# Two more head pairs and four raw weight pieces placed in layer 1's accumulators at the start, pieces in another order, first narrow unit behind the fourth pair

## The chip, the cores and the metric

One core of one Trainium2 chip runs the whole program. The metric is the device time of one execution in microseconds (us), as the median of several runs. Engines are named as in the profile: PE (TensorE matmul), PEld (its weight loads), DVE (VectorE), ACT (ScalarE), POOL (GpSimd), SP (the queue that issues nearly all DMAs).

## The reference, cut to what matters

A retention layer (attention without softmax, with a decay per head) feeds two feed-forward layers. The two layers' weights are float64, all else float32.

```python
# q, k, v: (4 batches, 8 heads, 576 tokens, 64), float32
scores = (1 / 8) * q @ k^T
D[i, j] = gamma[head] ** (i - j) if i >= j else 0
x = (scores * D) @ v                     # -> (2304 tokens, 512)
h = x @ w1_in;  g = max(0.01 * h, h);  x = g @ w1_out   # 512 -> 2048 -> 512
h = x @ w2_in;  g = h - tanh(h);       out = g @ w2_out
```

## The kernel before

**Retention** works on 16 head pairs (4 batches of 4 pairs; a pair fills the 128 partitions with 2 x 64). For pair i the four loads are `qT`, `kT` (288 KB each), `kn` (256 KB) and `vn` (320 KB), all issued by SP. Then: `prep(i)` on POOL scales the queries (L373) and the values (L378); `prep_tail(i)` on DVE scales the 64 last queries (L386), and ACT copies them into the tile `bd` (L390); `scores(i)` on PE (L401, L407) gives `sc` and `x_a`; `mask(i)` on DVE (L416, L423) turns these into `pt`; `states_mm(i)` on PE (L434) writes the products of each chunk into one PSUM tile `x_c`, and `states(i)` on ACT (L444) and DVE (L448, six instructions) adds them up with decay into `st`; `outputs_far` and `outputs_near` on PE (L465, L477) form the output from `st` and `pt`, in the PSUM tile `o` and, for the 64 last tokens, in a corner of `x_c`; `finish` splits the output into a high half `xh` (ACT, L486) and a low half `xl` (DVE, L487).

**Weights** come in pieces of 128 x 512 float64 (512 KB). A piece is loaded raw (`load_piece`, L109), narrowed to float32 by five steps (`narrow_ops`: an absolute value on ACT, L127; then on DVE a clamp, L137, a shift, L142, and two joins, L148), and split into a high and a low half (`split_piece`: ACT L174, POOL L175) in the tile `wp`. Two raw pieces fit in the pool `stage`, and two narrowed ones in the pool `cw` of this stage, so a third piece begins when the first has been split. The first eight pieces (four of layer 1's `w_in`, four of `w_out`) are narrowed during retention.

**Units.** From the sixth pair on, half of a block of 256 tokens of layer 1's first group is slipped in with each pair: `unit_h` (24 matmuls, L518, into the tile `x_b`), a leaky ReLU twice on ACT (L525, L526), the low half on POOL (L527), and `unit_o` (24 matmuls, L543), which is issued one pair later. There are 12 units. After every second one `unit_evac` copies sums into `acc`, an SBUF tile of 128 x 9216 float32 that accumulates layer 1's output. Until then `acc` holds nothing.

**Order.** No scheduler moves anything: each engine does its instructions in the order in which the code is written. In the loop over pairs it is load, prep of the next pair, scores, mask, prep_tail of the next pair, a part of the pieces' steps (`fill`), `pair_steps`, another part. The table `at_pair` says how many of the steps in the list `ops` are done by the end of each pair, a third of them at each of the up to three calls of `fill`. Behind retention `layers` runs layer 1's remaining blocks and layer 2, with PE as the engine that never rests (L194, L266).

Of the kernel before, what the change touches and what calls it, by code (L numbers as in the profile page):

```python
# [10 lines left out]
F32 = mybir.dt.float32  # L11
F32R = mybir.dt.float32r
U32 = mybir.dt.uint32
I64 = mybir.dt.int64
# [4 lines left out]
P = 128  # L19
# [14 lines left out]
def retention_moe_moe(  # L34
# [16 lines left out]
    nc = tc.nc  # L51
    B, NP, _, S = qT.shape
# [3 lines left out]
    NFULL = S // CH  # L56
    TAIL = S - NFULL * CH
    NCH = NFULL + 1
# [6 lines left out]
    stage = ctx.enter_context(tc.tile_pool(name="stage", bufs=2))  # L65
# [36 lines left out]
    cw_pool = [None]  # L102
    early = [True]

    def load_piece(key):
        m, kind, f = key
        src = ((w1i, w1o), (w2i, w2o))[m][kind][f]
        st = stage.tile([P, 512], I64 if wide else F32, tag="st", name="st")
        nc.sync.dma_start(out=st, in_=src)  # L109
        raw[key] = st  # L110

# [68 lines left out]
    def pieces_of(m, g):  # L180
        return [(m, kind, g * GF + f) for f in range(GF) for kind in range(2)]
# [125 lines left out]
    def split_order(keys):  # L307

        return sorted(keys, key=lambda k: (k[2] + LAG * k[1], k[1]))

    def piece_ops(keys, split=True, spare=()):


        ops, late = [], []
        for j, key in enumerate(keys):
            part = narrow_ops(key)
            if j + 2 < len(keys):
                part.append(lambda k=keys[j + 2]: load_piece(k))
            ops += part[:3] + late + part[3:]
            late = [lambda k=key: split_piece(k)] if split else []  # L320
            if key in spare:
                late = [lambda k=key: keep_piece(k)]
        return ops + late


    def retention():
        with ExitStack() as ac:
# [20 lines left out]
            qk, kv, pts = {}, {}, {}  # L348
            order = [(b, p) for b in range(B) for p in range(NP)]

            def load(i):
                load_qk(i)
                load_v(i)

            def load_qk(i):
                b, p = order[i]
                t = ap_.tile([P, 2, S], F32, tag="qk", name="qk")
                nc.sync.dma_start(out=t[:, 1, :], in_=qT[b, p])
                nc.sync.dma_start(out=t[:, 0, :], in_=kT[b, p])
                qk[i] = t  # L360

            def load_v(i):
                b, p = order[i]
                t = ap_.tile([P, NFULL + NCH, P], F32, tag="kv", name="kv")
                nc.sync.dma_start(out=t[:, :NFULL, :], in_=kn[b, p])
                nc.sync.dma_start(out=t[:, NFULL:, :], in_=vn[b, p])
                kv[i] = t
# [114 lines left out]
            def finish(i, ot):  # L482
                b, p = order[i]
                for src, lo, hi in ((o_tail, MAIN, S), (ot, 0, MAIN)):
                    ts = slice(b * S + lo, b * S + hi)
                    nc.scalar.activation(out=xh[:, p, ts], in_=src, func=AF.Copy)  # L486
                    nc.vector.tensor_tensor(  # L487
                        out=xl[:, p, ts], in0=src, in1=xh[:, p, ts].bitcast(F32), op=ALU.subtract
                    )


            pieces = split_order(pieces_of(0, 0))
            ops = piece_ops(pieces)
            at_pair = [3, 8, 14, 21, 30, 44, 54]
            first = NP + 1
            done, u = [0], 0

            def fill(i, part):
                a, b = ([0] + at_pair + [len(ops)] * len(order))[i:i + 2]
                now = a + (b - a) * (part + 1) // 3  # L500
                for op in ops[done[0]:now]:
                    op()
                done[0] = max(done[0], now)
# [7 lines left out]
            def unit_h(u):  # L511
                t0, f0 = place(u)
                for f in range(2):
                    w = wt[0, 0, f0 + f]
                    for kk in range(KK):
                        cs = slice(kk * P, (kk + 1) * P)
                        for j, (wi, x) in enumerate(((0, xh), (0, xl), (1, xh))):
                            nc.tensor.matmul(  # L518
                                out=x_b[:, f, :], lhsT=w[:, wi, cs], rhs=x[:, kk, t0:t0 + QW],
                                start=f == 0 and kk == 0 and j == 0,  # L520
                                stop=f == 1 and kk == KK - 1 and j == 2, skip_group_check=True,
                            )
                a = t0_.tile([P, 2, QW], F32, tag="u", name="a")
                gt = g0_.tile([P, 2, 2, QW], F32R, tag="g", name="g")
                nc.scalar.activation(out=a, in_=x_b, func=AF.Prelu, alpha=0.01)  # L525
                nc.scalar.activation(out=gt[:, 0], in_=x_b, func=AF.Prelu, alpha=0.01)  # L526
                nc.gpsimd.tensor_tensor(  # L527
                    out=gt[:, 1], in0=a, in1=gt[:, 0].bitcast(F32), op=ALU.subtract
                )
                gs[u] = gt  # L530

            def unit_o(u):
                t0, f0 = place(u)
                gt = gs.pop(u)
# [15 lines left out]

            def unit_evac(u):
                t0, f0 = place(u)
                if f0 == 0:
                    return
                ps = accs.pop(u // 2)
                dst = acc_t[:, :, t0:t0 + QW]
                nc.scalar.activation(out=dst[:, 2:], in_=ps[:, 2:], func=AF.Copy)
                nc.vector.tensor_copy(out=dst[:, :2], in_=ps[:, :2])

            def pair_steps(i, fast):  # L560

                nonlocal u
                if fast:
                    unit_h(u)
                    fill(i, 1)
                    if u:
                        unit_o(u - 1)
                        unit_evac(u - 1)
                    u += 1
                if i:  # L570
                    ot = outputs_far(i - 1)
                    outputs_near(i - 1, ot, [NFULL])
                    outputs_near(i - 1, ot, range(NFULL))
                    del pts[i - 1], kv[i - 1]
                if i < len(order):
                    states_mm(i)
                if i:
                    finish(i - 1, ot)
                if i < len(order):
                    states(i)  # L580

            t = ap_.tile([P, 2, S], F32, tag="qk", name="qk")
            nc.sync.dma_start(out=t[:, 1, :], in_=qT[0, 0])
            nc.scalar.dma_start(out=qt_sb[:, 0, :], in_=qtab[:, 0, :])
            nc.sync.dma_start(out=t[:, 0, :], in_=kT[0, 0])
            qk[0] = t
            nc.scalar.dma_start(out=cm_sb, in_=cmask)
            nc.scalar.dma_start(out=vt_sb, in_=vtab)
            nc.scalar.dma_start(out=qt_sb[:, 1:, :], in_=qtab[:, 1:, :])
            load_v(0)  # L590
            load_qk(1)
            load_piece(pieces[0])
            load_v(1)
            nc.vector.memset(qb[:, 2:3], 0.0)
            nc.vector.memset(qb[:, 0:1], -RHO_V * math.sqrt(RHO_C))
            nc.vector.memset(qb[:, 1:2], -TANH_T * TANH_T)
            nc.scalar.activation(out=qb[:, 3:4], in_=qb[:, 2:3], func=AF.Tanh)
            for t in sts + bds:
                nc.vector.memset(t, 0.0)
            load_piece(pieces[1])  # L600
            prep(0)
            prep_tail(0)
            for i in range(len(order)):
                if i + 2 < len(order):
                    load(i + 2)
                fast = i >= first
                if i + 1 < len(order):
                    prep(i + 1)
                sc = scores(i)
                scores_tail(i)  # L610
                mask(i, sc)
                if i + 1 < len(order):
                    prep_tail(i + 1)
                fill(i, 0)
                pair_steps(i, fast)
                fill(i, 2)
            pair_steps(len(order), True)
            assert done[0] >= len(ops)
            unit_o(u - 1)
            unit_evac(u - 1)  # L620
            assert 2 * u == n_early


    def layers():
# [135 lines left out]
```

## Time and profile before

| | before |
|---|---|
| median of 3 runs | 895.46 us (894.61 to 895.62) |
| profiled execution, first to last instruction (its span) | 893.7 us |
| what lies around the span, median less span | 1.8 us |
| PE busy | 868.6 us, 97% |
| DVE, ACT, POOL busy | 541.6, 378.0, 421.2 us |
| head of the program, 0 to 80 us: PE busy | 58.85 us |
| 80 to 160 us: PE busy | 80.00 us |
| 160 us to the end (733.7 us): PE busy | 729.75 us |

The profiled execution has only its span as a time of its own; a median belongs to it by adding the 1.8 us that lie around. Read the profile by stages: PE is busy without a gap from 80 us on, and nearly all of its idle time lies in the first 80 us, where the pairs and the first pieces are worked through. A row of the timeline gives start, duration, engine, line, operation, the tiles written and read, and in brackets how long the engine had been idle and what released it.

### The profile page before, as it was taken

To read this page: it belongs to the slowest core of one execution; us is meant where nothing else is said; L and a number is where in the kernel's file an instruction comes from. 1 tells how busy PE (TensorE), PEld (TensorE's weight loads), DVE (VectorE), ACT (ScalarE), POOL (GpSimd) and SP (SyncE) were. 2 spreads that over 40 slices of the span, in tenths; PEclk is the share of its full clock that TensorE was granted. 3 is DMA by queue.
4 is the path that set the end of the run, shared out by engine and by line. 5 is a ranking of instruction groups with operands and counts; after the bars stand their busy time and mean duration, and the time that the engine had idled before them with its cause. 6 is when DMAs were issued, how large, how long until landed. Compare 5 with 4: busy or idle time off the path is not lost.

```text
span 893.7 us, 13252 instructions
## 1 busy us (share of the span) xinstructions
PE 868.6 (97%) x5024; PEld 747.0 (84%) x5024; DVE 541.6 (61%) x922; ACT 378.0 (42%) x767; POOL 421.2 (47%) x340
## 2 busy tenths in 40 slices
PE   6869999999999999999999999999999999999998
PEld 5759999988888889888888888888888888888886
DVE  6864544698898787865662544444545555555454
ACT  2333232232222321232324666675566555565553
POOL 4544342265223622264224654585457744585443
PEclk9789999999999999999999999999999999999999
DMA  7634432132365335631120200020001000001111
GB/s 276 230 124 131 137 107 101 48 118 95 132 186 166 107 118 157 186 106 47 48 83 24 61 12 1 0 72 24 1 1 43 17 1 1 1 1 48 48 48 70
DMA packets 28574, 70.95 MB, mean 79 GB/s; under 512 B 3296, under 2 KB 3680, under 8 KB 28512
## 3 DMA queue, kind: packets, MB, share of 16 engines
q1 hardware_dynamic: 27936, 69.74, 23.7%
q8 instruction: 39, 0.64, 0.3%
q10 hardware_dynamic: 576, 0.38, 0.1%
q14 instruction: 23, 0.19, 0.1%
HBM read 59.10 MB, written 11.01 MB: 78 GB/s over the span
## 4 chain that ended last, share of the span: by engine, by line
PE 92%; DMA 2%; DVE 2%; POOL 1%; ACT 1%; issue 1%; SPq 0%; POOLq 0%; ACTq 0%
PE h L194 40%; PE a L266 40%; PE a L543 4%; PE x_b L518 3%; DMA kv<-in_vn 2%; PE sc L401 1%; PE o L477 1%; PE o L465 1%; POOL wp L175 1%; PE x_c L434 1%; PE x_a L407 0%; POOL kv L378 0%; DVE cw L148 0%; DVE cw L142 0%; PE x_c L477 0%
## 5 line engine op out<-in xcount | busy, mean ns | idle before, releaser
L194 PE MATMUL h<-xh,wp 128*128 128x512 f32 (+1 forms) x1184 | 355.3, 366 | 0.0
L194 PEld LDWEIGHTS h<-xh,wp 128*128 128x128 f32 x1184 | 216.1, 188 | 36.9
L194 PE MATMUL h<-xl,wp 128*128 128x512 f32 (+1 forms) x592 | 216.9, 366 | 0.0
L266 PE MATMUL a<-wp,g 128*128 128x512 f32 x864 | 209.4, 390 | 0.2 <-POOL g L240 0.2
L266 PEld LDWEIGHTS a<-wp,g 128*128 128x128 f32 x864 | 161.0, 188 | 33.8 <-POOL g L240 1.0
L266 PE MATMUL a<-g,wp 128*128 128x512 f32 (+1 forms) x816 | 175.6, 364 | 0.0
L240 POOL TENSOR_TENSOR g<-v,g 128x512 fp32r<-128x512 f32 (+1 forms) x80 | 94.9, 1186 | 144.6 <-ACT g L239 144.5
L266 PEld LDWEIGHTS a<-g,wp 128*128 128x128 f32 x816 | 141.4, 189 | 24.6
L240 POOL TENSOR_TENSOR g<-a,g 128x512 fp32r<-128x512 f32 (+1 forms) x68 | 87.5, 1286 | 154.5 <-ACT g L208 141.1
L207 ACT ACTIVATE a<-h 128x512 f32<-128x512 f32 (+1 forms) x68 | 37.3, 548 | 227.1 <-PE h L194 226.1
L175 POOL TENSOR_TENSOR wp<-cw,wp 128x512 fp32r<-128x512 f32 x64 | 91.1, 1432 | 82.8 <-ACT wp L174 82.5
L194 PEld LDWEIGHTS h<-xl,wp 128*128 128x128 f32 x592 | 111.6, 189 | 18.6
L233 DVE TENSOR_TENSOR h<-h,t 128x512 f32<-128x512 f32 (+1 forms) x80 | 51.5, 644 | 107.3 <-ACT t L217 107.3
L148 DVE SCALAR_TENSOR_TENSOR cw<-st,cw 128x512 uint32<-128x512 uint32 x128 | 113.3, 885 | 4.0
L292 DVE TENSOR_TENSOR acc<-a,acc 128x512 f32<-128x512 f32 (+1 forms) x114 | 74.0, 662 | 68.3 <-PE a L266 68.1
L239 ACT ACTIVATE g<-v 128x512 fp32r<-128x512 f32 (+1 forms) x80 | 47.2, 589 | 145.4 <-DVE v L237 144.3
L218 POOL TENSOR_TENSOR v<-t,u 128x512 f32<-128x512 f32 (+1 forms) x80 | 94.7, 1184 | 14.2 <-ACT t L217 13.8
L234 DVE SCALAR_TENSOR_TENSOR v<-q,v 128x512 f32<-128x512 f32 (+1 forms) x80 | 55.5, 694 | 55.2 <-POOL v L218 54.2
L237 DVE COPY_PREDICATED v<-mk,h 128x512 f32<-128x512 uint32 (+1 forms) x80 | 54.8, 685 | 9.2 <-DVE v L234 1.4
L219 ACT ACTIVATE q<-u,qb 128x512 f32<-128x512 f32 (+1 forms) x80 | 54.5, 681 | 0.0
L222 ACT ACTIVATE mk<-u,qb 128x512 f32<-128x512 f32 (+1 forms) x80 | 54.2, 678 | 0.0
L131 DVE TENSOR_SCALAR cw<-st 128x512 uint32<-128x512 uint32 x56 | 40.5, 724 | 18.6 <-DMA st<-in_w2i 6.4
(60 smaller groups left out, 803.7 us busy)
## 6 DMA issues: line engine op xcount, KB each, us to landing
st<-in_w1i SPq DMA_DIRECT2D x16, 512.0 KB, 3.3
st<-in_w1o SPq DMA_DIRECT2D x16, 512.0 KB, 3.2
st<-in_w2i SPq DMA_DIRECT2D x16, 512.0 KB, 3.8
st<-in_w2o SPq DMA_DIRECT2D x16, 512.0 KB, 3.8
kept<-cw SPq DMA_DIRECT2D x24, 256.0 KB, 4.1
cw<-kept SPq DMA_DIRECT2D x24, 256.0 KB, 2.6
kv<-in_vn SPq DMA_DIRECT2D x16, 320.0 KB, 5.2
qk<-in_qT SPq DMA_DIRECT2D x16, 288.0 KB, 3.4
```

Of the source, the lines that this page charges most:

```text
L148: nc.vector.scalar_tensor_tensor(out=t["w"], in0=t[src], scalar=scalar, in1=t["w"], op0=op, op1=ALU.bitwise_or)
L175: nc.gpsimd.tensor_tensor(out=wp[:, 1, :], in0=wf, in1=wp[:, 0, :].bitcast(F32), op=ALU.subtract)
L194: nc.tensor.matmul(out=ps[:, :n], lhsT=w[:, wi, cs], rhs=x[:, kk, t0:t0 + n], start=kk == 0 and i == 0, stop=kk == KK - 1 and i == 2,)
L218: nc.gpsimd.tensor_tensor(out=v[:, :n], in0=t_[:, :n], in1=u[:, :n], op=ALU.mult)
L219: nc.scalar.activation(out=q[:, :n], in_=u[:, :n], func=AF.Square, scale=math.sqrt(RHO_C), bias=qb[:, 0:1])
L222: nc.scalar.activation(out=mk[:, :n], in_=u[:, :n], func=AF.Relu, bias=qb[:, 1:2])
L233: nc.vector.tensor_tensor(out=h, in0=h, in1=t_, op=ALU.subtract)
L234: nc.vector.scalar_tensor_tensor(out=v, in0=q, scalar=RHO_A, in1=v, op0=ALU.add, op1=ALU.mult)
L237: nc.vector.copy_predicated(out=v, mask=mk.bitcast(U32), data=h)
L240: nc.gpsimd.tensor_tensor(out=gt[:, 1, :n], in0=v, in1=gt[:, 0, :n].bitcast(F32), op=ALU.subtract)
L266: nc.tensor.matmul(out=o, lhsT=l, rhs=r, start=f == 0 and i == 0 and d % pack == 0, stop=f == GF - 1 and i == 2 and (d + 1) % pack == 0, s ...
L292: nc.vector.tensor_tensor(out=dst, in0=a, in1=dst, op=ALU.add)
```

## The change

- Pairs 3 and 4 are loaded into `acc` (columns 4608 to 9215) and four raw pieces too (columns 0 to 4095), so that five pairs and six pieces are asked for at once at the start. `piece_ops` gets a parameter `ahead`: piece j + 6 is loaded behind piece j, where it was j + 2.
- In the loop pair i + 4 is loaded for i up to 1 and pair i + 2 after that, where the number is over 4. This names pair 5 twice, at i = 1 and at i = 3; both loads are issued, and the second is the one that is read.
- The pieces come as in 0, in 1, out 0, out 1, in 2, in 3, out 2, out 3; it was in 0, in 1, in 2, out 0, in 3, out 1, out 2, out 3.
- `at_pair` is 6, 12, 14, 18, 34, 50 (of 50 steps, loads among them); it was 3, 8, 14, 21, 30, 44, 54 (of 54).
- `first` is 4 in place of 5: the first `unit_h` stands with the fifth pair's states, behind the fourth pair's `finish`.
- `pair_steps` is in another order: outputs and `finish` of the last pair, `unit_o` and `unit_evac`, a part of the steps, then `states_mm` and `states`, then `unit_h`. It was `unit_h`, steps, `unit_o`, `unit_evac`, outputs, `states_mm`, `finish`, `states`. The `unit_o` that stood alone at the end of retention is gone into the loop's last `pair_steps`.

```diff
-    def load_piece(key):
+    def load_piece(key, at=None):
...
+        elif wide:
+            st = acc[:, at:at + 1024].bitcast(I64)
...
-            if j + 2 < len(keys):
-                part.append(lambda k=keys[j + 2]: load_piece(k))
+            if j + ahead < len(keys):
+                part.append(lambda k=keys[j + ahead]: load_piece(k))
...
+            homes = {3: (4608, 5760), 4: (6912, 8064)}
...
+                if i in homes:
+                    a = homes[i][0]
+                    t = acc[:, a:a + 2 * S].rearrange("p (s t) -> p s t", s=2)
...
-            pieces = split_order(pieces_of(0, 0))
-            ops = piece_ops(pieces)
-            at_pair = [3, 8, 14, 21, 30, 44, 54]
-            first = NP + 1
+            pieces = [(0, kind, f0 + f) for f0 in (0, 2) for kind in range(2) for f in range(2)]
+            ops = piece_ops(pieces, ahead=6)
+            at_pair = [6, 12, 14, 18, 34, 50]
+            first = NP
...
-            def pair_steps(i, fast):
+            def pair_steps(i):
                 nonlocal u
-                if fast:
-                    unit_h(u)
-                    fill(i, 1)
-                    if u:
-                        unit_o(u - 1)
-                        unit_evac(u - 1)
-                    u += 1
                 if i:
                     ot = outputs_far(i - 1)
                     outputs_near(i - 1, ot, [NFULL])
                     outputs_near(i - 1, ot, range(NFULL))
                     del pts[i - 1], kv[i - 1]
+                    finish(i - 1, ot)
+                if u:
+                    unit_o(u - 1)
+                    unit_evac(u - 1)
+                fill(i, 1)
                 if i < len(order):
                     states_mm(i)
-                if i:
-                    finish(i - 1, ot)
-                if i < len(order):
                     states(i)
+                    if i >= first:
+                        unit_h(u)
+                        u += 1
...
+            load_piece(pieces[0])
+            load(1)
+            load_piece(pieces[1])
+            load(2)
+            load(3)
+            load_piece(pieces[2], 0)
+            load_piece(pieces[3], 1024)
+            load(4)
+            load_piece(pieces[4], 2048)
+            load_piece(pieces[5], 3072)
...
-                if i + 2 < len(order):
-                    load(i + 2)
-                fast = i >= first
+                j = i + (2 if i > 1 else 4)
+                if 4 < j < len(order):
+                    load(j)
...
-                pair_steps(i, fast)
+                pair_steps(i)
                 fill(i, 2)
-            pair_steps(len(order), True)
+            pair_steps(len(order))
             assert done[0] >= len(ops)
-            unit_o(u - 1)
-            unit_evac(u - 1)
```

On PE, outputs of the first pair and what follows, before (`o` and `x_c` are the outputs' PSUM tiles; what stands in brackets are the semaphores waited for, DMAHW those of loads):

```order
L477 MATMUL x_c<-pt,kv 64x64 x2
L477 MATMUL o<-pt,kv 64x128 x8
L434 MATMUL x_c<-kv 64x64 [waits DMAHW4_49,DMAHW3_49,Pool_49]
L434 MATMUL x_c<-kv 64x64 x7
L401 MATMUL sc<-qk 128x128 [waits DMAHW6_49,DVE_49,DMAHW7_49,PE_49,Pool_49]
```

and in the changed kernel:

```order
L495 MATMUL x_c<-pt,kv 64x64 x2
L495 MATMUL o<-pt,kv 64x128 x8
L452 MATMUL x_c<-kv 64x64 [waits DMAHW3_49,DMAHW4_49,DVE_49,Pool_49]
L452 MATMUL x_c<-kv 64x64 x7
L419 MATMUL sc<-qk 128x128 [waits DMAHW6_49,DMAHW7_49,PE_49,Pool_49]
```

The chunk products of `states_mm` now wait for DVE: for the low half `xl<-x_c` of the pair before, which reads the corner of `x_c` and is written ahead of them now. The scores behind them have lost their own wait for DVE.

On DVE, from the mask of pair 1 to that of pair 2, before:

```order
L386 TENSOR_TENSOR qk<-qk,qt_sb 128x64 [waits DMAHW6_49]
L148 SCALAR_TENSOR_TENSOR cw<-st,cw 128x512 [waits DMAHW2_49,DVE_49]
L487 TENSOR_TENSOR xl<-x_c,xh 128x64 [waits Activation_49]
L487 TENSOR_TENSOR xl<-o,xh 128x512 [waits Activation_49]
L448 SCALAR_TENSOR_TENSOR st_100<-st_100,x_c 64x64 [waits Activation_49]
```

and in the changed kernel from the mask of pair 4 to that of pair 5 (line numbers are some 18 higher there):

```order
L404 TENSOR_TENSOR qk<-qk,qt_sb 128x64 [waits DMAHW4_49]
L153 SCALAR_TENSOR_TENSOR cw<-acc,cw 128x512 [waits DVE_49]
L142 TENSOR_SCALAR cw<-cw 128x512 [waits Activation_49]
L147 TENSOR_SCALAR cw<-cw 128x512 [waits DVE_49]
L505 TENSOR_TENSOR xl<-x_c,xh 128x64 [waits Activation_49]
L505 TENSOR_TENSOR xl<-o,xh 128x512 [waits Activation_49]
L153 SCALAR_TENSOR_TENSOR cw<-acc,cw 128x512 [waits DMAHW7_49,DVE_49]
L153 SCALAR_TENSOR_TENSOR cw<-acc,cw 128x512 [waits DVE_49]
L142 TENSOR_SCALAR cw<-cw 128x512 [waits Activation_49]
L147 TENSOR_SCALAR cw<-cw 128x512 [waits DVE_49]
```

Between the tail queries of the next pair and `xl<-x_c` there stood at most one step of a piece in the first pairs; in pairs 4 and 5 there are two or three now, and the clamp (L142) among them waits for ACT.

On SP, the loads between pairs 3 and 4 before (each waits for what frees its buffer):

```order
L109 DMA st<-in_w1i 128x512 [waits DMAHW6_49,DVE_49,Activation_49]
L358 DMA qk<-in_qT 128x576 [waits DMAHW7_49,PE_49,Pool_49]
L359 DMA qk<-in_kT 128x576 [waits DMAHW0_49]
L365 DMA kv<-in_kn 128x512 [waits DMAHW1_49,PE_49,Pool_49]
L366 DMA kv<-in_vn 128x640 [waits DMAHW2_49]
```

and the first loads that wait for more than another load in the changed kernel, 26 loads from the start:

```order
L114 DMA st<-in_w1o 128x512 [waits DMAHW6_49,DVE_49,Activation_49]
L369 DMA qk<-in_qT 128x576 [waits DMAHW7_49,PE_49,Pool_49]
L372 DMA qk<-in_kT 128x576 [waits DMAHW0_49]
L383 DMA kv<-in_kn 128x512 [waits DMAHW1_49,PE_49,Pool_49]
L384 DMA kv<-in_vn 128x640 [waits DMAHW2_49]
L114 DMA st<-in_w1o 128x512 [waits DMAHW3_49,DVE_49,Activation_49]
L369 DMA qk<-in_qT 128x576 [waits DMAHW4_49,PE_49,Pool_49]
```

The wait for PE and POOL has moved from the 15th load to the 28th. The second to fifth rows are pair 5's first load, the last row begins its second one. Not in these rows: the first piece stands ahead of pair 1's four loads now, where it stood between its `kT` and `kn`.

## Rows read from the trace of the kernel before

**Rows 1.** Windows: us, PE, PEld, DVE, ACT, POOL busy (instructions), clock, DMA share, GB/s.
```profile
0.00:80.00 80.00, 58.85 (x608) 53.55 (x609) 55.33 (x140) 27.15 (x71) 37.82 (x34) 0.89 0.58 199
```

**Rows 2.** Timeline of PE: first unit_h, stall in unit_o, end of second unit_o, scores.
```profile
39.89 0.56 PE L518 MATMUL x_b<-xh,wp 128*128 128x256 f32 x1
...
43.92 0.83 PE L465 MATMUL o<-qk,st 128*128 128x128 f32 x6
...
61.15 0.79 PE L543 MATMUL a<-g,wp 128*128 128x256 f32 x2 [5.70 <-ACT wp L174]
...
75.87 0.83 PE L465 MATMUL o<-qk,st 128*128 128x128 f32 x6
...
77.84 0.63 PE L434 MATMUL x_c<-kv 128*64 128x64 f32 x16
78.41 1.16 PE L401 MATMUL sc<-qk 64*128 64x128 f32 x16
```

**Rows 3.** Chain that ended last, in order of time: start, us, what.
```profile
79.99 2.87 PE x_b L518 x24
82.85 2.82 PE a L543 x24
89.63 2.87 PE x_b L518 x24
```

**Rows 4.** Waits of SP's queue, 0 to 80 us: us in total, times, longest.
```profile
SPq L109 <- DVE cw L148: 27.7, 6, 8.3
```

**Rows 5.** Timeline of DVE, masks (L416), piece steps, xl and states.
```profile
27.59 1.42 DVE L148 SCALAR_TENSOR_TENSOR cw<-st,cw 128x512 uint32<-128x512 uint32 x2
29.04 1.29 DVE L416 SCALAR_TENSOR_TENSOR pt<-sc,cm_sb 128x512 f32<-128x512 f32 x2
...
30.64 0.42 DVE L137 TENSOR_SCALAR cw<-cw 128x512 f32<-128x512 f32 x1
31.10 0.43 DVE L142 TENSOR_SCALAR cw<-cw 128x512 uint32<-128x512 uint32 x1
31.58 0.23 DVE L487 TENSOR_TENSOR xl<-x_c,xh 128x64 fp32r<-128x64 f32 x1
...
32.68 1.46 DVE L448 SCALAR_TENSOR_TENSOR st<-st,x_c 64x64 f32<-64x64 f32 x6
...
51.46 1.38 DVE L142 TENSOR_SCALAR cw<-cw 128x512 uint32<-128x512 uint32 x1
```

**Rows 6.** Timeline of ACT: tail copy, split, xh, states, absolute value; a late unit.
```profile
23.54 0.54 ACT L390 ACTIVATE bd<-qk 64x64 f32<-64x64 f32 x2 [4.94 <-DVE qk L386]
24.10 0.63 ACT L174 ACTIVATE wp<-cw 128x512 fp32r<-128x512 f32 x1
24.75 0.22 ACT L486 ACTIVATE xh<-x_c 128x64 fp32r<-128x64 f32 x1
...
25.35 0.45 ACT L444 ACTIVATE st<-x_c 64x64 f32<-64x64 f32 x2
26.10 0.67 ACT L127 ACTIVATE cw<-st 128x512 f32<-128x512 f32 x1 [0.30 <-POOL wp L175]
...
158.80 0.60 ACT L525 ACTIVATE a<-x_b 128x512 f32<-128x512 f32 x1 [2.07 <-PE x_b L518]
```

**Rows 7.** Timeline of POOL: values of pair 1, a split, low half of unit 11.
```profile
12.56 1.26 POOL L378 TENSOR_TENSOR kv<-kv,vt_sb 128x640 f32<-128x640 f32 x1 [2.03 <-DMA kv<-in_vn]
...
51.19 1.36 POOL L175 TENSOR_TENSOR wp<-cw,wp 128x512 fp32r<-128x512 f32 x1
...
160.02 1.30 POOL L527 TENSOR_TENSOR g<-a,g 128x512 fp32r<-128x512 f32 x1 [7.03 <-ACT g L526]
```

**Rows 8.** Windows, columns as in rows 1: full load queue; before and in the first unit_h.
```profile
10.50:16.20 5.70, 5.61 (x54) 5.27 (x56) 3.85 (x13) 0.99 (x3) 2.57 (x3) 1.00 0.97 360
...
36.00:38.00 2.00, 0.23 (x9) 0.10 (x4) 1.97 (x5) 0.00 (x0) 1.31 (x2) 1.00 0.23 59
...
40.00:42.00 2.00, 2.00 (x12) 2.00 (x11) 1.61 (x7) 1.25 (x4) 1.96 (x2) 0.50 0.99 352
```

More of the change, by code (lines that the diff above doesn't have):

```diff
@@ L103, in retention_moe_moe @@
     early = [True]
-    def load_piece(key):
+    def load_piece(key, at=None):
         m, kind, f = key
         src = ((w1i, w1o), (w2i, w2o))[m][kind][f]
-        st = stage.tile([P, 512], I64 if wide else F32, tag="st", name="st")
+        if at is None:
+            st = stage.tile([P, 512], I64 if wide else F32, tag="st", name="st")
+        elif wide:
+            st = acc[:, at:at + 1024].bitcast(I64)
+        else:
+            st = acc[:, at:at + 512]
         nc.sync.dma_start(out=st, in_=src)
@@ L309, in split_order, with piece_ops @@
         return sorted(keys, key=lambda k: (k[2] + LAG * k[1], k[1]))
-    def piece_ops(keys, split=True, spare=()):
+    def piece_ops(keys, split=True, spare=(), ahead=2):
         ops, late = [], []
@@ L356, in load_qk @@
                 b, p = order[i]
-                t = ap_.tile([P, 2, S], F32, tag="qk", name="qk")
+                if i in homes:
+                    a = homes[i][0]
+                    t = acc[:, a:a + 2 * S].rearrange("p (s t) -> p s t", s=2)
+                else:
+                    t = ap_.tile([P, 2, S], F32, tag="qk", name="qk")
                 nc.sync.dma_start(out=t[:, 1, :], in_=qT[b, p])
+                if i == 0:
+                    nc.scalar.dma_start(out=qt_sb[:, 0, :], in_=qtab[:, 0, :])
                 nc.sync.dma_start(out=t[:, 0, :], in_=kT[b, p])
@@ L363, in load_v @@
                 b, p = order[i]
-                t = ap_.tile([P, NFULL + NCH, P], F32, tag="kv", name="kv")
+                n = NFULL + NCH
+                if i in homes:
+                    a = homes[i][1]
+                    t = acc[:, a:a + n * P].rearrange("p (c d) -> p c d", c=n)
+                else:
+                    t = ap_.tile([P, n, P], F32, tag="kv", name="kv")
                 nc.sync.dma_start(out=t[:, :NFULL, :], in_=kn[b, p])
@@ L574, in pair_steps @@
                     del pts[i - 1], kv[i - 1]
+                    finish(i - 1, ot)
[3 more added lines that the diff above has]
+                fill(i, 1)
                 if i < len(order):
                     states_mm(i)
-                if i:
-                    finish(i - 1, ot)
-                if i < len(order):
                     states(i)
[L582 to L586, printed above, removed]
+                    if i >= first:
+                        unit_h(u)
+                        u += 1
+            load_qk(0)
             nc.scalar.dma_start(out=cm_sb, in_=cmask)
@@ L599, in retention @@
                 nc.vector.memset(t, 0.0)
-            load_piece(pieces[1])
             prep(0)
@@ L614, in retention @@
                 fill(i, 0)
-                pair_steps(i, fast)
+                pair_steps(i)
                 fill(i, 2)
-            pair_steps(len(order), True)
+            pair_steps(len(order))
             assert done[0] >= len(ops)
-            unit_o(u - 1)
-            unit_evac(u - 1)
-            assert 2 * u == n_early
+            assert u == n_early // 2
     def layers():
```

2 lines of the change are left out of this document (removed).

## The prediction

> **What bounds the kernel now.** I read the windows by stage first, then PE's timeline in the first 80 us, then those of the other engines. PE is busy 58.85 of the first 80 us [rows 1], and from 80 us on it never rests (the table ahead), so all that this change can give lies in those 21 us of idle time; what stands behind just moves along. The longest hole is the one of 5.70 us in the first `unit_o` at 61.15 [rows 2]: the splits of the piece out 1 and of the next came late. From the end of the second `unit_o`, at 75.87, the flow is steady: a pair with its unit takes 89.63 - 79.99 = 9.64 us, of which `unit_h` is 2.87 and `unit_o` 2.82 [rows 3], outputs 77.84 - 75.87 = 1.97, chunk products 0.57 [rows 2], and scores the other 1.41.
>
> So I compare both kernels at one mark, the end of the second `unit_o`. Before it is at 75.87, but PE has by then done one pair's scores and chunk products and one `unit_h` more than the changed order has at that mark: 1.41 + 0.57 + 2.87 = 4.85 us. A changed kernel that reaches the mark at **71.0 us** is even.
>
> **What holds the first pairs is no load but a chain over DVE, ACT and POOL.** In the changed order each pair's chunk products wait for the low half `xl<-x_c` of the pair before, and this stands on DVE behind the mask and behind piece steps that wait for ACT, where the copy of the next pair's tail (`bd`) stands ahead of them. I walk this chain with rows. DVE: masks with tail queries 30.64 - 29.04 = 1.60 us, clamp 0.46 and shift 0.48 from start to start, a join 1.42 / 2 = 0.71, `xl<-x_c` 0.23, states 1.46 [rows 5]. ACT: `bd` 0.54, split 0.63, `xh` 0.22, first state 0.45, absolute value 0.67 [rows 6]. POOL: 1.30 [rows 7]. For a step from engine to engine I take 0.1 us, to PE 0.2, an estimate from unit 11: POOL begins 1.22 us after the first of two overlapping ACT copies of 0.60 [rows 6, 7].
>
> **Mask of pair 1.** The first piece now stands ahead of pair 1's `qT`, so this comes later. Pair 1's `vn` closes the same sum of bytes in both orders and landed at 12.56 [rows 7]; `qT` stands 288 + 256 + 320 = 864 KB ahead of it, 2.5 us at 360 GB/s [rows 8], so 10.1. Then tail queries 0.2 (an estimate), `bd`, absolute value, clamp, shift, join, states, join with hops: 0.2 + 0.1 + 0.54 + 0.67 + 0.1 + 0.46 + 0.48 + 0.71 + 1.46 + 0.71 = 5.4. Start **15.5**.
>
> **Mask of pair 2.** 1.60 + 0.1 + `bd` 0.54 + absolute value 0.67 + 0.1 + clamp 0.46 + `xl` 0.23 + 0.2 + chunk products 0.57 + 0.1 + 0.45 + 0.1 + states 1.46 + two joins 1.42 = 8.0 us. A piece step that begins while POOL works is stretched: the shift at 51.46 took 1.38 us in place of 0.43 and ended 0.29 us behind POOL's instruction of 51.19 [rows 5, 7]. POOL does a split and two multiplies in a row here, so I add 0.9: 8.9, **24.4**.
>
> **Mask of pair 3.** No DVE step of a piece is here: 1.60 + 0.1 + 0.54 + `xh` 0.22 + 0.1 + 0.23 + 0.2 + 0.57 + 0.1 + 0.45 + 0.1 + 1.46 = 5.7. PE works about 4 us in each such pair and stands for the rest. Before, the clock was 0.50 (1.2 GHz) in 40 to 42 us, after PE had been busy 0.23 us of 36 to 38 [rows 8]; the products then take double. I add 0.4: 6.1, **30.5** (before: 29.04 [rows 5]).
>
> **Mask of pair 4.** The same 5.7 and a join 0.71; 0.8 because outputs at the lower clock hold the products, 0.5 for one stretched step: 7.7, **38.2**.
>
> **First unit.** 1.60 + 0.1 + 0.54 + 0.67 + split 0.63 + 0.22 + 0.1 + 0.23 + 0.2 = 4.3, chunk products at the lower clock 1.1: `unit_h` starts at **43.6**, where before it started at 39.89, and takes 43.92 - 39.89 = 4.03 as it did then [rows 2] (2.87 at full clock): end 47.6.
>
> **The two pairs with 16 steps each.** Mask 5 stands behind clamp and shift of a piece that waits for a buffer of `cw`, and this for POOL's split behind POOL's low half of the unit: 0.1 + 1.22 + 1.30 + 1.30 + 0.1 + 0.67 + 0.1 + 0.46 + 0.48 = 5.7, with 0.5 for stretching 6.2: **53.8**. PE meanwhile does scores, outputs and the first `unit_o`, 1.41 + 1.97 + 2.82 = 6.2, with no wait, and is done at 53.8. Then the chunk products wait for mask, `bd`, a split on ACT and POOL, absolute value, clamp, `xl`: 1.60 + 0.1 + 0.54 + 0.63 + 0.1 + 1.30 + 0.1 + 0.67 + 0.1 + 0.46 + 0.23 + 0.2 = 6.0, so at **59.8**: a hole of 6.0 us on PE in place of that of 5.70. Behind it, at the lower clock: products 1.1, `unit_h` 4.03, scores 1.41, outputs 1.97, `unit_o` 2.82 and 0.3 for its last split: 11.6. The mark is reached at **71.4**, 0.4 us late.
>
> **What else.** At the end `unit_h` 11 now has only the outputs, 1.97 us, between it and its `unit_o`; its low half is ready 0.1 + 160.02 + 1.30 - 158.80 = 2.6 us behind it [rows 6, 7]: 0.6 us of wait, where the tenth `unit_o` covered it. The loads cost nothing: up to pair 5's second `qT` the queue moves, behind pair 1's `vn`, pairs 2 to 5 once (4,608 KB), seven pieces (3,584 KB) and that `qT` (288 KB), 8.7 MB or 24 us at 360 GB/s [rows 8]; it lands at about 36.7, and it is asked for at 39.8, behind mask 4. That cover of 3 us is gone if the queue runs at 320 GB/s. The 50 steps are the 54 less four loads issued earlier. In the steady flow `xl` is hidden by `unit_o` (2.82 us against mask, `bd` and `xh`, 2.6, which run beside outputs too): nothing.
>
> Sum: +0.4 + 0.6 = **+1.0 us**. The profiled execution's span goes from 893.7 to 894.7, and with the 1.8 us around it the median from 895.46 to **896.5**.
>
> **Bounds.** Nothing stretched: -0.9 - 0.5 - 0.5 = -1.9. Full clock all the way: -0.4 - 0.8 - 0.5 - 1.2 - 0.5 - 1.2 = -4.6. Together 890.0. On the other side stretching in each place where POOL works beside (0.5 more in pair 4, 0.7 before mask 5, 1.0 before the second unit, 0.3 behind it): +2.5, 899.0. I stay near the middle, since the rows show the lower clock behind a hole as well as full clock [rows 8], and a stretched step (1.38) as well as unstretched ones (0.43) [rows 5].
>
> **Rivals.** *The late data was the bound.* SP waited 27.7 us for DVE to free raw buffers [rows 4]; with the pieces there, splits come early, PE's holes are short, and the clock stays up: the low end, **890.0**. For it speaks the hole of 5.70 us; against it that SP's waits follow DVE's pace and don't set it. Trace Analysis of the Trainium skill (section Optimization Strategy) says that a repeated gap on the engine that should be saturated can mean too few buffers for the next tile; by that rule more room gives the whole gain. The trace agrees only for the raw pieces: DVE, which frees them, is busy 55.33 of the 80 us.
>
> *Piece steps and POOL hold each other.* 32 DVE steps on 8 pieces now lie closer to splits and multiplies; each meeting costs 1.38 - 0.43 = 0.95 us on a chain that PE now waits for. This ends at **899.0**, slower, and decides from a first `unit_h` that starts later than 44.4 (0.8 us behind my 43.6 is +1.8). SBUF — State Buffer of the Trainium skill (section Who interferes with whom) says that DVE and GpSimd share a port pair as an exclusive lock, so that the second one waits for the first to finish; the row of 51.46 agrees, and by the rule alone each such meeting counts whole, which is this rival's time and not the 1.9 us of my sum.
>
> *The change doesn't do what it says.* Pair 5 is loaded twice, and only the second load is used, so the room won ahead of it is not used for it: 1,152 KB or 3.3 us of queue. At 280 GB/s its `qT` lands near 43.6, 3.8 us behind need, of which the steps ahead of `bd` hide about half: **898.4**.
>
> **How the numbers follow.** A measurement of this kernel tells 0.2%, 1.8 us, from no change. My sum 0.40 (same 0.31, slower 0.06, faster 0.03), data 0.30 (faster), port 0.22 (slower 0.20, same 0.02), double load 0.08 (slower 0.06, same 0.02): faster 0.33, same 0.35, slower 0.32. The range must reach to both sides: 889.5 to 899.0; my own case alone spans 894 to 898.
>
> **What would show it.** First `unit_h` at 43 to 44.5 us, at half clock; a hole of 5 to 6.5 us on PE ahead of the sixth pair's chunk products, ended by DVE's `xl`; the second `unit_o` ends near 71.4; a wait of 0.6 us ahead of the last `unit_o`; PE full between. It is wrong if the first unit starts by 41 us, if those products find `xl` done, or if PE waits for a load.

## The result, and the profile after

| | before | after |
|---|---|---|
| median | 895.54 us (894.61 to 897.89, 4 runs) | 905.61 us (904.56 to 906.45, 4 runs) |
| ratio, 95% interval | | 1.0108, 1.0094 to 1.0123 |
| span of the profiled execution | 893.7 us | 904.4 us |
| PE busy | 868.6 us | 876.0 us |

The change makes the kernel slower by 10.1 us; 896.5 was forecast, with a range of 889.5 to 899.0. The spans differ by 10.7 us, and all of it lies in retention: the first matmul of the stage behind it starts at 177.09 us, where before it started at 166.36. From there to the end both kernels take 727.3 us.

The windows of after (columns as in [rows 1]) show where PE has no work.

```profile
0.00:80.00 80.00, 56.17 (x536) 50.93 (x538) 54.67 (x132) 24.84 (x64) 34.62 (x30) 0.87 0.57 206
80.00:160.00 80.00, 80.00 (x868) 74.57 (x865) 42.15 (x108) 23.95 (x68) 29.85 (x24) 1.00 0.37 118
```

In the first 80 us PE is busy 56.17 us, 2.7 less than before [rows 1]. From 80 to 160 us it is busy all of the time, as before; by this number nothing is lost there. PE's timeline shows something else. First the head, with the places that the prediction named:

```profile
45.33 1.12 PE L452 MATMUL x_c<-acc 128*64 128x64 f32 x16 [4.23 <-issue]
46.38 0.58 PE L536 MATMUL x_b<-xh,wp 128*128 128x256 f32 x1
...
62.68 1.12 PE L452 MATMUL x_c<-kv 128*64 128x64 f32 x16 [5.71 <-DVE xl L505]
63.73 0.58 PE L536 MATMUL x_b<-xh,wp 128*128 128x256 f32 x1
...
72.60 3.21 PE L561 MATMUL a<-g,wp 128*128 128x256 f32 x24
75.75 0.69 PE L452 MATMUL x_c<-kv 128*64 128x64 f32 x16
```

The first `unit_h` (L536) starts at 46.38 us (before 39.89 [rows 2]); the hole ahead of the sixth pair's chunk products (L452) is 5.71 us; the second `unit_o` (L561), the mark of the prediction, ends at 75.75, where 71.0 would be even. The head thus loses 4.7 us. The hole of 4.23 us ahead of the fifth pair's products names no releaser ("issue" is idle time for which the profile shows no wait); in the run without POOL's scaling, below, the same hole is 4.19 us and DVE's `xl` ends it.

Now one steady pair, in before and then in after. The shape behind the tiles is that of the weights (rows*columns), then the output.

```profile
79.74 0.36 PE L518 MATMUL x_b<-xh,wp 128*128 128x256 f32 x1
...
82.69 2.98 PE L543 MATMUL a<-g,wp 128*128 128x256 f32 x24
85.51 0.83 PE L465 MATMUL o<-qk,st 128*128 128x128 f32 x6
...
87.48 0.63 PE L434 MATMUL x_c<-kv 128*64 128x64 f32 x16
88.05 1.16 PE L401 MATMUL sc<-qk 64*128 64x128 f32 x16
...
89.38 0.36 PE L518 MATMUL x_b<-xh,wp 128*128 128x256 f32 x1
```

```profile
86.58 0.39 PE L536 MATMUL x_b<-xh,wp 128*128 128x256 f32 x1
...
89.64 1.16 PE L419 MATMUL sc<-qk 64*128 64x128 f32 x16
...
91.05 0.83 PE L483 MATMUL o<-qk,st 128*128 128x128 f32 x6
...
92.15 1.05 PE L495 MATMUL o<-pt,kv 128*64 128x128 f32 x16
93.13 3.11 PE L561 MATMUL a<-g,wp 128*128 128x256 f32 x24
96.17 0.69 PE L452 MATMUL x_c<-kv 128*64 128x64 f32 x16
96.78 0.39 PE L536 MATMUL x_b<-xh,wp 128*128 128x256 f32 x1
```

From `unit_h` to `unit_h` it takes 96.78 - 86.58 = 10.20 us; before it took 89.38 - 79.74 = 9.64. No row names a wait. From start to start `unit_h` takes 3.06 us (2.95 before), scores 1.41 (1.33), outputs 2.08 (1.97), `unit_o` 3.04 (2.82), products 0.61 (0.57). The chunk products start at 75.75 in the mark's pair and at 167.61 in the last: nine periods, 91.86 us, against 9 x 9.65 before, **+5.0 us**. PE's weight loads ahead of `unit_o` show one place where it happens, in after and then in before:

```profile
92.48 0.47 PEld L495 LDWEIGHTS o<-pt,kv 128*64 128x64 f32 x8
93.12 0.65 PEld L561 LDWEIGHTS a<-g,wp 128*128 128x128 f32 x5 [0.17 <-issue]
```

```profile
92.10 0.19 PEld L518 LDWEIGHTS x_b<-xh,wp 128*128 128x128 f32 x1
92.22 0.78 PEld L543 LDWEIGHTS a<-g,wp 128*128 128x128 f32 x6
```

Ahead of `unit_o` the loading of weights stands still in after for 0.17 us and waits for nothing that the profile knows. Before, `unit_o` stood behind `unit_h`, whose weights have the same shape, and its first weights were loaded under `unit_h`'s last products, with no pause (92.22 is ahead of 92.10 + 0.19).

The end of retention has the wait that the prediction named, 0.63 us ahead of the last `unit_o`:

```profile
174.28 2.96 PE L561 MATMUL a<-g,wp 128*128 128x256 f32 x23 [0.63 <-POOL g L545]
```

Together: head 4.7, nine periods 5.0, the end of retention 1.0 (that wait of 0.63; the rest I put down to changes of shape): 10.7 us.

### The profile page after: what moved, and what is told of

Read it like the earlier page. It is cut to its first block, busy times and chain, and to the rows that moved or that the text cites. A ratio compares the mean times of both kernels' runs of the same rounds, so it can differ in the third digit from the quotient of the medians.

```text
span 904.4 us, 13265 instructions
## 1 busy us (share of the span) xinstructions
PE 876.0 (97%) x5024; PEld 750.0 (83%) x5024; DVE 552.2 (61%) x922; ACT 379.4 (42%) x767; POOL 422.1 (47%) x340
## 4 chain that ended last, share of the span: by engine, by line
PE 92%; issue 3%; POOL 2%; DMA 1%; ACT 1%; DVE 1%; SPq 0%; POOLq 0%; ACTq 0%
PE h L199 40%; PE a L271 40%; PE x_b L536 4%; PE a L561 3%; PE sc L419 1%; PE o L483 1%; PE o L495 1%; PE x_c L452 1%; DMA qk<-in_qT 1%; PE x_a L425 1%; POOL wp L180 0%; DMA qt_sb<-in_qtab 0%; POOL acc L391 0%; PE x_c L495 0%; POOL qk L391 0%
## 5 line engine op out<-in xcount | busy, mean ns | idle before, releaser
L153 DVE SCALAR_TENSOR_TENSOR cw<-st,cw 128x512 uint32<-128x512 uint32 x120 | 109.0, 909 | 3.8
L221 ACT ACTIVATE u<-h 128x512 f32<-128x512 f32 (+1 forms) x80 | 43.7, 546 | 18.9 <-PE h L199 18.5
```

The source lines that it names most:

```text
L153: nc.vector.scalar_tensor_tensor(out=t["w"], in0=t[src], scalar=scalar, in1=t["w"], op0=op, op1=ALU.bitwise_or)
```

## Experiments

Three theories for the steady pair: PE loses time each time it changes between weights of another shape (128*128, the 128*64 of products and near outputs, the 64*128 of scores); or it pays for new waits; or the data's new place is the cause. For the head: DVE and POOL holding each other, the pool of narrowed pieces, the loads.

### The order alone

```diff
 # before
-    unit_h(u) ; fill ; unit_o(u - 1) ; unit_evac(u - 1)
     outputs(i - 1)
-    states_mm(i) ; finish(i - 1) ; states(i)
+    finish(i - 1) ; unit_o(u - 1) ; unit_evac(u - 1) ; fill
+    states_mm(i) ; states(i) ; unit_h(u)
```

> The kernel before with one thing changed: the order inside pair_steps is that of the changed kernel (outputs, finish, unit_o, steps, chunk products, states, unit_h); units still start with the sixth pair, data and pieces as before. Switch theory: in the changed kernel PE loses 0.56 us in each steady pair because its blocks with 64-wide weights and its blocks with full 128x128 weights now alternate more often, and the first weights of a block of the other width are not loaded under the block ahead. It expects a period of 10.2 us in place of 9.64 from the second unit on, 10 times, +5.6, and the wait of 0.6 to 1.0 ahead of the last unit_o; with nothing more in the head 901.5 to 903.5. Placement theory (the loss comes with the data in the accumulators and the pieces' order): period 9.64, 895.5 to 897.

Measured: 907.03 us, ratio 1.0132 (1.0113 to 1.0150). The period is 10.21 us from the second unit on (products at 86.21 and at 96.42, for one), with data, pieces and steps as before: placement is out. The time is higher than expected because of the last unit, which has nothing left between `unit_h` and `unit_o` here:

```profile
171.12 0.39 PE L543 MATMUL a<-g,wp 128*128 128x256 f32 x1 [1.24 <-ACT g L526]
172.51 5.28 PE L543 MATMUL a<-g,wp 128*128 128x256 f32 x23 [1.01 <-POOL g L527]
```

Behind two waits of 2.25 us in all, this `unit_o` ran at a granted clock of 0.50 (1.2 GHz) and took 5.28 us.

### Two changes of shape more, and no new wait

```diff
 # before, from the sixth pair on
     unit_h(u)
     fill(i, 1)
+    states_mm(i)
     unit_o(u - 1)
...
     outputs(i - 1)
-    states_mm(i)
```

> The kernel before with the chunk products of a pair (64-wide weights) issued between unit_h and unit_o in place of behind the outputs, from the sixth pair on; no instruction of PE waits for anything later than it did. Switch theory: two more changes of width in each steady pair (into the products and out of them), 0.25 to 0.35 us each pair, 11 pairs, +3 to +4: 898.5 to 899.5, period 9.9 to 10.0. Wait theory (the 0.56 us are the new waits, products behind DVE's low half and unit_o behind the outputs): period 9.64, time 895 to 896.

Measured: 896.75 us, ratio 1.0016 (1.0003 to 1.0029), and a period of 10.01 us, as the theory of shapes has it:

```profile
80.63 0.69 PE L434 MATMUL x_c<-kv 128*64 128x64 f32 x16
81.25 3.12 PE L543 MATMUL a<-g,wp 128*128 128x256 f32 x24
...
90.65 0.69 PE L434 MATMUL x_c<-kv 128*64 128x64 f32 x16
```

No instruction of PE waits for more than it did, and yet each pair costs 0.37 us more. The total was forecast too high, for the head became shorter: the seventh pair's products run at 55.46 us in place of 67.46, ahead of the first `unit_o` and not behind it and its hole of 5.70 us [rows 2]. That this is the reason is read from the order; no run tests it apart.

### A control: a block of the same shape in the same place

```diff
 # before, from the eighth pair on
     scores(i)
+    unit_h(u)
     scores_tail(i)
     mask(i)
...
-    unit_h(u)
     unit_o(u - 1)
```

> A control on the kernel before: from the eighth pair on, the two matmuls of the tail's scores (x_a, full 128x128 weights) stand between unit_h and unit_o in place of ahead of unit_h. PE has as many block boundaries more as in a run with the chunk products there, but the same number of changes between 64-wide and full weights (scores to unit_h in place of scores to x_a). Theory of the width: period 9.64 within 0.06, time 895 to 896.5. Rival (any small block put between unit_h and unit_o costs the 0.37 us that the chunk products cost there): period 9.9 to 10.0 in 9 pairs, +2.5 to +3.5.

Measured: 895.59 us, ratio 0.9998 (0.9986 to 1.0010), period 9.67 (`unit_h` at 100.22 and at 109.89).

```profile
100.22 0.39 PE L518 MATMUL x_b<-xh,wp 128*128 128x256 f32 x1
...
103.20 0.38 PE L407 MATMUL x_a<-bd,qk 128*128 128x128 f32 x2
103.33 3.09 PE L543 MATMUL a<-g,wp 128*128 128x256 f32 x24
```

A block put between the two units costs next to nothing (0.02 us) if its weights have their shape. It is the shape, not the boundary.

### One change taken back

```diff
 # after
     outputs(i - 1)
+    states_mm(i) ; finish(i - 1) ; states(i)
-    finish(i - 1)
     unit_o(u - 1) ; unit_evac(u - 1) ; fill
-    states_mm(i) ; states(i)
     unit_h(u)
```

> The changed kernel with the chunk products and states of a pair put directly behind the outputs, ahead of finish, and unit_o and unit_h one behind the other after them. Switch theory: two changes of width fewer in each steady pair, period 10.21 to about 9.9, 9 or 10 times, -2.4 to -3; the products no longer wait for the low half, but unit_h does, so the head gains 0 to 2: 901 to 903. If the period stays at 10.2 the loss is not the changes of width; if it falls to 9.64 at once it was the wait of the products.

Measured: 900.24 us, ratio 1.0053 (1.0035 to 1.0072), period 9.84:

```profile
80.52 0.63 PE L452 MATMUL x_c<-kv 128*64 128x64 f32 x16
...
90.36 0.63 PE L452 MATMUL x_c<-kv 128*64 128x64 f32 x16
```

The second `unit_o` ends at 74.17 us with the pair's products (0.57) already done, so the head gained 75.75 - 74.17 + 0.57 = 2.2, and nine periods gave 9 x 0.37 = 3.3. The time is 0.8 us below the range that was expected; the period fell as forecast.

The five orders side by side; counted are changes of the weights' shape within one pair:

| order | changes | period, us |
|---|---|---|
| before | 3 (scores to `x_a`, far to near outputs, products to scores) | 9.65 |
| `x_a` between the units | 3 | 9.67 |
| after, products first | 4 | 9.84 |
| before, products between the units | 5 | 10.01 |
| after, and its order alone | 6 | 10.21 |

Each change costs (10.21 - 9.65) / 3 = **0.19 us**, and the row for 4 and that for 5 lie on the same line. With blocks of three shapes no order has fewer than three.

### Pair 5 loaded once

```diff
 # after
-    if 4 < j < len(order):
+    if 4 < j < len(order) and i != 3:
         load(j)
```

> The changed kernel with pair 5 loaded once, at the second pair, in place of twice. My theory (loads cost nothing): 905.6 within 1 us. Rival, the second load of pair 5 holds up the head: 902 to 903.5, and the first unit_h starts 1 to 3 us earlier than 46.38.

Measured: 905.71 us, ratio 1.0111 (1.0096 to 1.0127): no difference. The first `unit_h` starts at 45.33 in the profiled execution, 1.05 us earlier, which just meets the rival's sign. But 0.49 us of it is there at the mask of pair 1 already (16.21 for 16.70), which starts anywhere from 15.8 to 16.7 us in the runs of kernels with these steps of pieces, and this execution was the fastest of the four (904.71); the median is not in the rival's range.

### Early data alone

```diff
 # after, with the order, first unit and order of pieces of before
-    at_pair = [6, 12, 14, 18, 34, 50]
-    first = NP
+    at_pair = [3, 8, 14, 20, 28, 40, 50]
+    first = NP + 1
```

> The kernel before (its order, its order of pieces, its steps per pair, first unit with the sixth pair) with only the data early: pairs 3 and 4 and four raw pieces in the accumulators, six pieces and five pairs asked for at the start. My theory (the head is held by the chain over DVE, ACT and POOL, not by loads; early data only lets POOL scale pairs ahead and meet DVE's joins): 895 to 898. Rival, the late data was the bound of the head: about 890, with the hole of 5.70 us ahead of the first unit_o shorter by more than 3 us.

Measured: 896.72 us, ratio 1.0012 (1.0001 to 1.0022). The rival that the late data was the bound falls: the first `unit_o` still waits for its splits, and the first of them releases it at 62.54, where it did so at 61.15 before [rows 2]. The hole itself is shorter by 5.70 - 2.91 = 2.79 us, close to the rival's sign, but nothing is won by it: a hole of 3.01 us now stands ahead of the second `unit_h` (0.88 before), and the second `unit_o` ends at 77.06 in place of 75.87.

```profile
62.54 0.50 PE L561 MATMUL a<-g,wp 128*128 128x256 f32 x2 [2.91 <-ACT wp L179]
```

### POOL's scaling of three pairs taken away

```diff
 # after
     def prep(i):
+        if i in (2, 3, 4):
+            return
```

> The changed kernel without POOL's scaling of queries and values of the pairs 2, 3 and 4 (left out, so these pairs' output is not scaled rightly). Theory of meetings (POOL, which has its data early, works next to DVE's piece steps and stretches them: two joins 3.16 us in place of 1.42, ahead of the mask of pair 2): joins back at about 1.4, mask of pair 2 at 25 to 25.5 in place of 27.13, first unit_h 1.5 to 2.5 us earlier than 46.38, time 903 to 904.5. Rival (the joins only wait in line with the rest of the chain): first unit_h stays within 0.5 us and the time at 905.6.

Measured: 903.34 us, ratio 1.0088 (1.0073 to 1.0103), 2.3 us less than after. DVE in after, then in this kernel:

```profile
12.94 1.63 DVE L153 SCALAR_TENSOR_TENSOR cw<-st,cw 128x512 uint32<-128x512 uint32 x1
...
21.02 1.51 DVE L147 TENSOR_SCALAR cw<-cw 128x512 uint32<-128x512 uint32 x1
...
23.94 3.16 DVE L153 SCALAR_TENSOR_TENSOR cw<-st,cw 128x512 uint32<-128x512 uint32 x2
27.13 1.29 DVE L434 SCALAR_TENSOR_TENSOR pt<-sc,cm_sb 128x512 f32<-128x512 f32 x2
```

```profile
23.00 1.42 DVE L153 SCALAR_TENSOR_TENSOR cw<-st,cw 128x512 uint32<-128x512 uint32 x2
24.45 1.29 DVE L436 SCALAR_TENSOR_TENSOR pt<-sc,cm_sb 128x512 f32<-128x512 f32 x2
```

What POOL did meanwhile in after:

```profile
20.97 1.27 POOL L180 TENSOR_TENSOR wp<-cw,wp 128x512 fp32r<-128x512 f32 x1 [2.65 <-ACT wp L179]
22.20 1.45 POOL L391 TENSOR_TENSOR acc<-acc,qt_sb 128x512 f32<-128x512 f32 x1
23.61 1.26 POOL L396 TENSOR_TENSOR acc<-acc,vt_sb 128x640 f32<-128x640 f32 x1
24.83 1.72 POOL L391 TENSOR_TENSOR acc<-acc,qt_sb 128x512 f32<-128x512 f32 x1
26.51 1.70 POOL L396 TENSOR_TENSOR acc<-acc,vt_sb 128x640 f32<-128x640 f32 x1
```

Five POOL instructions follow each other with no pause, those of pairs 3 and 4 back to back, because the data of both is there. Two joins take 3.16 us beside them and 1.42 without, and the shift 1.51 in place of 0.43 (the split at 20.97 is its neighbour). The mask of pair 2 comes 2.7 us earlier without the scaling; about 0.9 of that is the earlier mask of pair 1 (15.78 in this run), the rest the joins. The mask of pair 2 itself also starts beside a multiply of POOL (26.51 to 28.21) and takes 1.29 us as it does without: not every step of DVE is stretched. The first `unit_h` starts at 42.92 us, 3.5 earlier, more than expected, and some of this is lost again behind it: the clamp ahead of the mask of pair 5 waits 4.91 us in place of 3.77, and the second `unit_o` ends 2.8 us earlier, at 72.93.

### A third buffer for narrowed pieces

```diff
 # after
-    cw_pool[0] = ac.enter_context(tc.tile_pool(name="c0", bufs=2))
+    cw_pool[0] = ac.enter_context(tc.tile_pool(name="c0", bufs=3))
-    qt_sb = ak.tile([P, NP, CH], F32, name="qt_sb")
+    qt_sb = acc[:, 4096:4096 + NP * CH].rearrange("p (n c) -> p n c", n=NP)
```

> The changed kernel with three narrowed pieces at a time in the pool of the retention stage in place of two (the query table lies in free columns of the accumulators to make room). Theory: the mask of pair 5 (57.11) is late because a clamp waits 3.77 us for an absolute value that waits for a buffer, that is for POOL's split behind POOL's low half of the first unit; with a third buffer it starts 2 to 3 us earlier, the hole of 5.71 us on PE shortens by as much: 902.5 to 904. Rival (DVE's and POOL's work is the bound there, not the buffer): 905 to 906. The steady period stays at 10.2 us by either.

Measured: 901.94 us, ratio 1.0072 (1.0055 to 1.0089), 3.7 us less than after by the medians (2.7 by the spans of the profiled executions, 901.7 and 904.4), a little more than expected. ACT and DVE ahead of the mask of pair 5, in after:

```profile
54.18 0.68 ACT L132 ACTIVATE cw<-acc 128x512 f32<-128x512 f32 x1 [2.10 <-POOL wp L180]
54.89 0.79 DVE L142 TENSOR_SCALAR cw<-cw 128x512 f32<-128x512 f32 x1 [3.77 <-ACT cw L132]
...
57.11 1.29 DVE L434 SCALAR_TENSOR_TENSOR pt<-sc,cm_sb 128x512 f32<-128x512 f32 x2
```

And with three buffers, with PE's row behind it:

```profile
51.97 0.68 ACT L132 ACTIVATE cw<-acc 128x512 f32<-128x512 f32 x1
...
54.65 1.29 DVE L434 SCALAR_TENSOR_TENSOR pt<-sc,cm_sb 128x512 f32<-128x512 f32 x2
60.09 1.12 PE L452 MATMUL x_c<-kv 128*64 128x64 f32 x16 [3.12 <-DVE xl L505]
```

The absolute value follows the split before it at once, the mask starts 2.5 us earlier, the hole on PE is 3.12 us in place of 5.71, and the second `unit_o` ends at 72.99, 2.8 us earlier.

### Both taken back

The diff is that of "one change taken back" and that of the third buffer together, on after.

> The changed kernel with two of its costs taken back together: chunk products and states directly behind the outputs with unit_o and unit_h in a row, and three narrowed pieces at a time. Apart the two gave -5.4 (905.6 to 900.2) and -3.7 (905.6 to 901.9). If they are separate costs, 896 to 898; if both shorten the same holes of the head, of the -5.4 only the steady part stays (0.37 us in each of 9 pairs and the rest of the order's tail), 898.5 to 900.5.

Measured: 896.14 us, ratio 1.0010 (1.0000 to 1.0021). The two costs are separate: 5.4 + 3.7 = 9.1 us apart, 9.5 together (by the spans of the profiled executions 8.4 and 10.4). The period is 9.84 here too, so some 0.2 x 9 us of the order's cost are still in it, and by this count the early pieces and the earlier first unit win no more than that back.

### One pair of before in another order

```diff
 # before, seventh pair only
-    unit_h(u) ; fill ; unit_o(u - 1) ; unit_evac(u - 1)
     outputs(i - 1) ; states_mm(i) ; finish(i - 1) ; states(i)
+    unit_h(u) ; fill ; unit_o(u - 1) ; unit_evac(u - 1)
```

> The kernel before with one pair's steps in another order, those of the seventh pair, where unit_h of the second unit and unit_o of the first wait for splits: outputs, chunk products, finish and states of that pair go ahead of the two. Theory: PE does 2.5 us of outputs and products inside the holes of 0.88, 0.94 and 5.70 us, and DVE goes on with the pieces; the second unit_o ends 1.5 to 2.5 us earlier than 75.87: 893 to 894. Rival (the pieces' chain sets the end whatever PE does in the holes, or the steps behind states come later): 895 to 896.5.

Measured: 893.02 us (889.93 to 893.46), ratio 0.9965 (0.9954 to 0.9976): **faster than both kernels**.

```profile
56.15 1.62 PE L465 MATMUL o<-qk,st 128*128 128x128 f32 x6 [6.62 <-DVE st L448]
...
73.48 0.83 PE L465 MATMUL o<-qk,st 128*128 128x128 f32 x6
```

The size came out as expected, the way there did not: PE does no work inside the old holes. There is one hole of 6.62 us ahead of the outputs, which DVE's states end, and then both units run without a pause. Before, the holes of this stretch add up to 0.88 + 0.94 + 5.70 + 0.56 + 0.45 = 8.5 us, the longest of them in [rows 2]. The second `unit_o` ends at 73.48 in place of 75.87.

### The same with a third buffer

> The kernel before with the seventh pair's outputs, products, finish and states ahead of unit_h and unit_o, and with three narrowed pieces at a time (query table in free columns of the accumulators). If the buffer is worth in this order what it is in the other (an absolute value no longer waits for POOL's split), the hole of 6.62 us on PE shortens by 1 to 3 us: 890 to 892. If DVE's line of masks, states and piece steps sets that hole, as its long joins say, the buffer gives nothing: 892.5 to 893.5.

Measured: 891.94 us (890.92 to 893.67), ratio 0.9959 (0.9943 to 0.9975). The hole stays:

```profile
55.79 1.62 PE L465 MATMUL o<-qk,st 128*128 128x128 f32 x6 [6.61 <-DVE st L448]
```

By its median the run falls into the first forecast (890 to 892), by its hole into the second. The intervals of the two kernels overlap, and the spans (891.9 and 891.3) say nothing for the buffer, so no gain is shown. The hole has the same length and the same releaser with either number of buffers: in this order it is DVE's line of steps that sets it, and not the buffer.

## Why the prediction was wrong

**The step that failed is "In the steady flow ... nothing".** It asked only whether `xl` is in time, and took each block of PE at the length that it had in the old order: 9.64 us was cut into `unit_h`, `unit_o`, outputs, products and scores, and these parts were put together anew. I never asked what the parts' lengths owe to their neighbours. The new order has six changes of shape where the old has three, 10.21 - 9.65 = 0.56 us in each pair, 5.0 us in nine. That is the larger part of the 9.7 us by which the span exceeds its forecast (904.4 for 894.7); the walk through the head gives 4.35 and the end of retention 0.4. The Trainium skill states the rule, under TensorEngine Tiling (Array Packing), section Key Properties: a change of the tiling mode, not of the tile alone, drains TensorE. The periods of these runs agree and give it its price. It was a rule that speaks against this change, and the prediction weighed another one.

**"PE full between"** was right by the busy time (80.00 of 80 us) and wrong in what I took it for. Time lost at a change counts as busy: in after, the row of the near outputs lasts from 92.15 to 93.20 us, over the 0.17 us up to 93.12 in which no weights load. Periods show the loss, and so do the instructions and PEld's busy time in a window. The row of before for 80 to 160 us, with the same columns as the windows of after:

```profile
80.00:160.00 80.00, 80.00 (x899) 78.07 (x899) 35.25 (x113) 23.96 (x68) 27.93 (x22) 1.00 0.34 110
```

899 matmuls where after has 868, and 78.07 us of weight loads where after has 74.57.

**The walk through the head** was 4.35 us too short at the mark (75.75 for 71.4). By its steps, forecast and measured, in us:

| step | forecast | measured |
|---|---|---|
| start of mask of pair 1 | 15.5 | 16.70 |
| to mask of pair 2 | 8.9 | 10.43 |
| to mask of pair 3 | 6.1 | 6.09 |
| to mask of pair 4 | 7.7 | 7.96 |
| to first `unit_h` | 5.4 | 5.20 |
| to mask of pair 5 | 10.2 | 10.73 |
| to the sixth pair's chunk products | 6.0 | 5.57 |
| to the end of the second `unit_o` | 11.6 | 13.07 |

Five of the eight steps hold within 0.55 us, and so do the hole (6.0 for 5.71) and its releaser. Two terms were too small. Stretching by POOL was booked with 0.9 us ahead of mask 2; the two joins alone lost 3.16 - 1.42 = 1.74, the shift 1.08, and one join ahead of mask 1 another 0.9 (1.63 for 0.71). That two pairs' scaling would run in a row was in the order, and I counted "a split and two multiplies". The rival of piece steps and POOL named this, with the point from which it decides (a first `unit_h` later than 44.4; it came at 46.38); its 899.0 is short by the 5.0 us of the steady flow and by 1.9 of the head. SBUF — State Buffer of the Trainium skill (section Who interferes with whom) would have counted each meeting whole, and the trace agrees with that for the joins, 1.74 us for two of them against the 0.95 of one meeting. As a rule for every meeting it is too wide: the mask of pair 2 began beside a multiply of POOL and was not stretched.

The second term is the clock. The second `unit_h` took 69.11 - 63.73 = 5.38 us in place of 4.03, all of it at half clock:

```profile
57.00:62.70 5.70, 0.02 (x2) 0.02 (x2) 3.65 (x11) 2.46 (x7) 1.26 (x1) 0.95 0.00 0
...
63.70:69.10 5.40, 5.40 (x26) 5.20 (x24) 5.08 (x12) 1.02 (x3) 0.81 (x1) 0.51 0.00 0
```

PE had been busy 0.02 of the 5.70 us ahead; I had taken the 4.03 of the first unit before, part of which ran at full clock (granted clock 0.50 in 40 to 42 us [rows 8], 0.91 in 42 to 44).

None of the three signs of being wrong that the prediction names came true: the first unit started late, the products did not find `xl` done, and PE waited for no load there. All three stand in the head, and none looks at the length of a steady pair.

**What was right:** the wait of 0.6 us ahead of the last `unit_o` (0.63); that loads cost nothing, pair 5's second load among them (905.71 without it); that the late data was not the bound (896.72 with the data alone); that the buffer of `cw` holds the mask of pair 5 (3.7 us with a third).

**Open:** how much of the head's 4.7 us belongs to the new wait of the chunk products for `xl`, apart from the chain behind it. With products first that wait is gone and the head gains 2.2 us, but the order of DVE's steps changes with it. Also open is what within a change of shape takes the 0.19 us: the runs count changes, and only one of them, ahead of `unit_o`, was followed to a pause of the weight loads.

## What to carry to other kernels

Count the changes of the weights' shape on PE per turn of a loop before its blocks are put in another order: blocks of one shape belong next to each other, and a part's length from the old order holds only with its old neighbours. A PE that shows 100% busy can still lose 6%; compare the period of a loop, not the busy share. Data that comes early lets another engine run early too; ask first which steps on a shared path it will then meet.

## What the runs showed of the hardware that was not expected

A change between weights of 128*128, 128*64 and 64*128 costs PE 0.19 us at full clock, over orders with 3, 4, 5 and 6 of them per pair (9.65, 9.84, 10.01, 10.21 us); ahead of `unit_o`, the weight load behind such a change starts late with no wait shown (0.17 us "issue"). And a short pause can cost more than itself: behind waits of 1.24 and 1.01 us the last `unit_o` of the run with the order alone ran at 1.2 GHz and took 5.28 us, while behind 0.63 us in after it ran at 2.4 GHz and took 2.96.
